# One of two subtractions of the query items handed from VectorE to ScalarE and GpSimd, in eight items of a transformer block

## The chip, the cores and the metric

The kernel runs on one core of a Trainium2 chip. The metric is the device time of one execution in microseconds (us); a time without more words is the median of several runs. The core has five engines that run side by side, each through its own instructions in order: TensorE (PE; its weight loads are shown apart as PEld), VectorE (DVE), ScalarE (ACT), GpSimd (POOL) and SyncE (SP), which here only issues DMAs. ScalarE issues some DMAs too. They wait for one another by semaphores.

## What is computed

The reference is one transformer block on 2048 rows of 1024 values, in float32: a layer norm, linear attention with a learned feature map, a projection, and a ReLU network with 3584 hidden values, each with its residual. The change touches the feature map of the queries:

```python
pq = jnp.einsum("bhsd,hdf->bhsf", q, w_phi)
phi_q = jnp.concatenate([_softmax(pq, axis=-1), _softmax(-pq, axis=-1)], axis=-1)
...
num = jnp.einsum("bhqf,bhfd->bhqd", phi_q, kv)
den = jnp.einsum("bhqf,bhf->bhq", phi_q, z)[..., None] + 1e-6
```

There are 32 heads with 32 features each. A softmax over the 32 scores of a head needs exp(score - maximum), the softmax of the negated scores needs exp(minimum - score).

## The kernel before, in words

**Tiles and stages.** The rows are 16 tiles of 128. Every product is made of three matmuls (`mm3`, L182 to L184), since each operand is held as a rounded part and a rest: `Units` takes a weight from DRAM, ScalarE copies it (L125), and GpSimd or VectorE subtracts the copy from the raw weight (L129). The weights lie in a ring of ten places (`w`); a place is free when the matmuls of the last step that reads it are over. An item is one output tile of 128x512, eight steps of three matmuls. The order of items is: for each half of the tiles (0 to 7, then 8 to 15) 32 key and value items, 8 query items with s = 0 (the first 16 heads) and 8 with s = 1; then the projection of the attention (`wo_item`), and the network (`up_item`, `down_item`). The query items of the second half with s = 0 are items 80 to 87 of the program; those with s = 1 are 88 to 95.

**A query item.** `q_first` runs behind its last matmul. VectorE takes the maximum and the minimum of each head's 32 scores from PSUM (L516, L517, tile `qmx`), then writes score less maximum (L520) and minimum less score (L521) into the halves of tile `qe`, 128 x 1024, of which there are two buffers. Then come, at steps given by hand, `q_second` (ScalarE: the exponential of the whole tile, L525, and two DMAs of it to DRAM, L529, tensor `ed`), `q_third` (VectorE: sums L534 and reciprocals L535, tile `qsm`) and `q_fourth` (GpSimd: two small products, L544, tile `smq`).

**The attention.** 32 units u, each four row tiles of two heads' groups, are read back from `ed` in another order (`at_load`) and go through GpSimd, VectorE and ScalarE: `at_sums` (GpSimd, L595, tile `ez`), `at_reduce` (VectorE, L602, `qtz`), `at_cross` (ScalarE, L613), `at_den` (GpSimd, L617 and L618), `at_inverse` (VectorE, L621), `at_scale` (GpSimd, L626 for the first six units, L631 for the others), `at_turn` (VectorE, a transpose, L637). For the first six units the sums are made earlier. After two units `at_num` makes 32 short matmuls (L650), which need the transposes of both units, and ScalarE and VectorE take the result from PSUM (L657, L667). This work is spread by hand over the items from 83 on.

**What sets the order.** `when(step, f, ...)` puts a piece of work behind a step; step 8 n + k is step k of item n. At each step the pieces run in the order in which they were put there, and then `W.advance` starts the loads and splits of weights that have a free place. Every engine goes through its own instructions in exactly this order. So `q_second` of item n stands at step 6 of item n + 1, `q_third` at step 3 of item n + 2, `q_fourth` at step 3 of item n + 3. Of the units, `at_scale` of units 0, 1 and 2 stands at step 4 of item 85, step 5 of item 86 and step 7 of item 87, that of unit 3 at step 0 of item 89; `at_num` of the first pair stands at step 5 of item 88.

**A ring of weights.** While item 87 runs, the weights of the items with s = 1 come into the ring: step k of item 87 frees the place for weight k + 2, and ScalarE (L125) and GpSimd (L129) make it. Item 88 reads weight k at its step k, its rest first in the matmul of L183. The weights of the projection follow with a slower pace, by turns from GpSimd and VectorE (L129 both).

Of the kernel before, what the change touches and what calls it, by code (L numbers as in the profile page):

```python
# [11 lines left out]
AF = mybir.ActivationFunctionType  # L12
ALU = mybir.AluOpType
AX = mybir.AxisListType

P = 128
# [6 lines left out]
HT = NT // 2  # L23
# [117 lines left out]
def kernel(  # L141
# [12 lines left out]
    v, act, pool, pe, sp = nc.vector, nc.scalar, nc.gpsimd, nc.tensor, nc.sync  # L154
# [34 lines left out]
    def do(n, k, f, *args):  # L189
        at[n, k].append((f, args))  # L190
# [230 lines left out]
    e_of, v_of, phi_of, kv_ps, kd_of = {}, {}, {}, {}, {}  # L421
# [85 lines left out]
    def q_item(s, t, keys):  # L507
        ps = yield from project(t, keys)
        q_first(s, t, ps)

    def q_first(s, t, ps):

        pq = ps.rearrange("p (h f) -> p h f", f=32)
        pa = ps.rearrange("p (a c f) -> p a c f", a=4, c=4)
        m = pqp.tile([P, 2, 16], F32, name="qmx", bufs=2)
        v.tensor_reduce(out=m[:, 0, :], in_=pq, op=ALU.max, axis=AX.X)  # L516
        v.tensor_reduce(out=m[:, 1, :], in_=pq, op=ALU.min, axis=AX.X)  # L517
        e = pqp.tile([P, 4, 2, 4, 32], F32, name="qe", bufs=2)
        m = m.rearrange("p s (a c) -> p s a c", a=4)
        v.tensor_sub(e[:, :, 0], pa, m[:, 0, :, :, None].to_broadcast([P, 4, 4, 32]))  # L520
        v.tensor_sub(e[:, :, 1], m[:, 1, :, :, None].to_broadcast([P, 4, 4, 32]), pa)  # L521
        e_of[s, t] = e

    def q_second(s, t):
        act.activation(e_of[s, t], e_of[s, t], AF.Exp)  # L525
        b, i = place_of[t]
        dst = ed[b].rearrange("a i (g s t) (n x) -> s (i g) (t n) a x", g=2, s=2, n=4)
        for sd in range(2):
            act.dma_start(dst[sd, i, :, 4 * s:4 * s + 4], e_of[s, t].rearrange("p a s c f -> s p a (c f)")[sd])  # L529
# [417 lines left out]
    def item(gen, *args, keys):  # L947
        items.append((gen, args + (keys,)))
        steps.extend((k,) for k in keys)
        return len(items) - 1  # L950
# [11 lines left out]
    for b, tiles in enumerate(groups):  # L962
        for hf in range(2):

            pairs = b == 0 and hf == 0
            for j in range(0, 4, 2 if pairs else 1):
# [3 lines left out]
                for half in range(2):  # L970
                    n = item(wo_pair, tiles[j:j + 2], hf, half, keys=[("wo", hf, 4 * half + k // 2) for k in range(8)])
# [26 lines left out]
    def when(step, f, *args):  # L998

        if step < 8 * first_up:  # L1000
            do(step // 8, step % 8, f, *args)
        else:
            do(first_up + (step - 8 * first_up) // 4, step % 4, f, *args)
# [4 lines left out]
    for t in range(1, NT):  # L1008
        n = t - 1 if t < HT else q_n[1, t - HT] + 1
# [104 lines left out]

    a0 = last_kv + 6
    for (sl, t), n in q_n.items():
        when(8 * n + 14, q_second, sl, t)
        when(8 * n + 19, q_third, sl, t)
        when(8 * n + 27, q_fourth, sl, t)
        b, i = place_of[t]  # L1120
        if (sl, i) == (1, 3):
            when(8 * n + 34, sm_store, b)
            when(8 * n + (48, 48, 48, 72)[b], sm_load, b)
# [88 lines left out]
    for b in range(2):  # L1212
        for m in DOWN:
            n = down_n[b, m, NP - 1] + 1
# [110 lines left out]
```

## Time and profile before

| | us |
|---|---|
| median of 3 runs | 1872.5 (1872.37 to 1872.6) |
| the profiled execution | 1870.48 |
| its span, first to last instruction | 1868.7 |
| mean granted clock of TensorE | 0.999 of full speed |

A line of a timeline gives the start in us, the duration, the engine, the line of the kernel, the operation, what it writes and reads, and how many instructions are merged; in brackets stands how long the engine was idle before, and what released it. A line of the waits names who waited for whom: us in total, times, the longest. A line of the stretches has for each engine the busy us and in brackets the instructions, then the granted clock, the DMAs' busy share and GB/s. The durations of matmuls overlap, since the next one starts before the one ahead has ended; what counts is the distance of their starts.

### The profile page before, as it was taken

To read this page: it belongs to the slowest core of one execution; us is meant where nothing else is said; L and a number is where in the kernel's file an instruction comes from. 1 tells how busy PE (TensorE), PEld (TensorE's weight loads), DVE (VectorE), ACT (ScalarE), POOL (GpSimd) and SP (SyncE) were. 2 spreads that over 40 slices of the span, in tenths; PEclk is the share of its full clock that TensorE was granted. 3 is DMA by queue.
4 is the path that set the end of the run, shared out by engine and by line. 5 is a ranking of instruction groups with operands and counts; after the bars stand their busy time and mean duration, and the time that the engine had idled before them with its cause. 6 is when DMAs were issued, how large, how long until landed. Compare 5 with 4: busy or idle time off the path is not lost.

```text
span 1868.7 us, 28840 instructions
## 1 busy us (share of the span) xinstructions
PE 1856.5 (99%) x10064; PEld 1516.3 (81%) x10064; DVE 1063.8 (57%) x1655; ACT 770.5 (41%) x1379; POOL 979.0 (52%) x991
## 2 busy tenths in 40 slices
PE   9999999999999999999999999999999999999999
PEld 7777788888887777888888888888888888888887
DVE  7787678677689878575555653443433333343333
ACT  5322245233333333354455554444444444444442
POOL 4887745888947988343333222222344444444443
PEclk9999999999999999999999999999999999999999
DMA  7988798666575676887888975666677677777765
GB/s 229 286 294 288 231 289 270 190 203 202 178 227 181 223 243 203 280 278 232 247 262 259 324 249 184 193 201 205 225 223 215 216 218 239 238 215 217 216 216 177
DMA packets 333635, 433.04 MB, mean 232 GB/s; under 512 B 28720, under 2 KB 194608, under 8 KB 333488
## 3 DMA queue, kind: packets, MB, share of 16 engines
q1 hardware_dynamic: 299696, 414.41, 70.1%
q10 hardware_dynamic: 33792, 16.78, 3.2%
q8 instruction: 79, 1.29, 0.3%
q14 instruction: 68, 0.56, 0.1%
HBM read 293.21 MB, written 137.89 MB: 231 GB/s over the span
## 4 chain that ended last, share of the span: by engine, by line
PE 93%; DVE 3%; POOL 1%; issue 1%; ACT 0%; DMA 0%; SPq 0%; ACTq 0%; DVEq 0%; POOLq 0%
PE mm L182 24%; PE mm L183 24%; PE mm L184 24%; PE ac L182 4%; PE ac L184 4%; PE ac L183 4%; PE tp L184 2%; PE tp L183 2%; PE tp L182 2%; PE tp L246 1%; PE ac L465 1%; PE ac L650 1%; DVE qsm L534 0%; DVE qe L637 0%; POOL w L129 0%
## 5 line engine op out<-in xcount | busy, mean ns | idle before, releaser
L129 POOL TENSOR_TENSOR w<-raw,w 128x512 fp32r<-128x512 f32 x353 | 469.0, 1331 | 698.3 <-ACT w L125 663.2
L125 ACT ACTIVATE w<-raw 128x512 fp32r<-128x512 f32 x686 | 409.4, 626 | 508.8 <-PE mm L184 232.4
L129 DVE TENSOR_TENSOR w<-raw,w 128x512 fp32r<-128x512 f32 x333 | 271.0, 815 | 511.6 <-ACT w L125 507.6
L182 PE MATMUL mm<-w,xT 128*128 128x512 f32 x768 | 306.0, 398 | 0.0
L183 PE MATMUL mm<-w,xT 128*128 128x512 f32 x768 | 300.2, 391 | 0.4 <-POOL w L401 0.4
L184 PE MATMUL mm<-w,xT 128*128 128x512 f32 x768 | 299.6, 390 | 0.0
L182 PE MATMUL mm<-hT,w 128*128 128x512 f32 x672 | 261.5, 389 | 0.0
L183 PE MATMUL mm<-hT,w 128*128 128x512 f32 x672 | 261.5, 389 | 0.0
L184 PE MATMUL mm<-hT,w 128*128 128x512 f32 x672 | 261.5, 389 | 0.0
L182 PEld LDWEIGHTS mm<-w,xT 128*128 128x128 f32 x768 | 144.4, 188 | 35.2 <-issue 4.1
L184 PEld LDWEIGHTS mm<-w,xT 128*128 128x128 f32 x768 | 144.4, 188 | 30.9
L363 POOL TENSOR_TENSOR b<-b 128x256 f32<-128x256 f32 x176 | 143.6, 816 | 48.0 <-DMA b<-in_w_dram 38.6
L183 PEld LDWEIGHTS mm<-w,xT 128*128 128x128 f32 x768 | 144.6, 188 | 29.2 <-POOL w L401 1.0
L184 PE MATMUL mm<-w 128*128 128x512 f32 x392 | 152.6, 389 | 0.0
L182 PE MATMUL mm<-w 128*128 128x512 f32 x392 | 152.6, 389 | 0.0
L183 PE MATMUL mm<-w 128*128 128x512 f32 x392 | 152.6, 389 | 0.0
L182 PEld LDWEIGHTS mm<-hT,w 128*128 128x128 f32 x672 | 126.2, 188 | 26.4
L183 PEld LDWEIGHTS mm<-hT,w 128*128 128x128 f32 x672 | 126.2, 188 | 26.2
L184 PEld LDWEIGHTS mm<-hT,w 128*128 128x128 f32 x672 | 126.2, 188 | 26.0
L183 PEld LDWEIGHTS mm<-w 128*128 128x128 f32 x392 | 73.6, 188 | 15.3
L184 PEld LDWEIGHTS mm<-w 128*128 128x128 f32 x392 | 73.6, 188 | 15.2
L182 PEld LDWEIGHTS mm<-w 128*128 128x128 f32 x392 | 73.6, 188 | 15.3
(173 smaller groups left out, 3106.0 us busy)
## 6 DMA issues: line engine op xcount, KB each, us to landing
raw<-t SPq DMA_DIRECT2D x224, 256.0 KB, 3.9
raw<-ad SPq DMA_DIRECT2D x196, 256.0 KB, 3.0
raw<-in_w_dram SPq DMA_DIRECT2D x168, 256.0 KB, 3.1
ad<-c SPq DMA_DIRECT2D x112, 256.0 KB, 3.6
b<-in_w_dram SPq DMA_DIRECT2D x44, 512.0 KB, 5.8
t<-b SPq DMA_DIRECT2D x44, 512.0 KB, 5.0
ad<-s SPq DMA_DIRECT2D x84, 256.0 KB, 4.1
ed<-qe ACTq DMA_DIRECT2D x64, 256.0 KB, 4.1
```

Source lines behind the costliest of these rows:

```text
L125: nc.scalar.activation(w[:, 0, :], raw[1], AF.Copy)
L129: eng.tensor_tensor(out=w[:, 1, :], in0=raw[1], in1=w[:, 0, :].bitcast(F32), op=ALU.subtract)
L182: pe.matmul(ps, a_hi, b_hi, start=first, stop=False, skip_group_check=more)
L183: pe.matmul(ps, a_hi, b_lo, start=False, stop=False, skip_group_check=more)
L184: pe.matmul(ps, a_lo, b_hi, start=False, stop=last, skip_group_check=more)
L246: pe.transpose(pt[:, k, :], xn[:, (4 * j + k) * P:(4 * j + k + 1) * P], ident)
L363: pool.tensor_tensor(out=tsum[*u, *out], in0=tsum[*u, *a], in1=tsum[*u, *b], op=ALU.subtract)
L465: pe.matmul(kv_ps[s][g][32 * i:32 * (i + 1), 0:64], vt[:, 32 * h:32 * (h + 1)], phi[:, 64 * h:64 * (h + 1)], start=first, stop=last)
L650: pe.matmul(banks[g][32 * c:32 * (c + 1), 256 * j:256 * (j + 1)], kvL[rows, 2 * q + h // 4, 32 * (h % 4):32 * (h % 4 + 1)], phT_of[u - 1 + ...
```

## The change

In the items 80 to 87 VectorE no longer makes minimum less score. ScalarE copies the scores from PSUM into the second half of `qe` with factor -1, behind the other instructions of `q_first`. GpSimd then adds the minimum, repeated over the 32 features, in place. This addition is a new piece `q_min`, at step 8 n + 12, that is at step 4 of item n + 1, two steps ahead of the exponential. At that step it is put ahead of what other loops put there and ahead of the weights that the step frees. The eight other items of the second half, and all of the first half, stay as they are.

```diff
         v.tensor_sub(e[:, :, 0], pa, m[:, 0, :, :, None].to_broadcast([P, 4, 4, 32]))
-        v.tensor_sub(e[:, :, 1], m[:, 1, :, :, None].to_broadcast([P, 4, 4, 32]), pa)
         e_of[s, t] = e
+        if t >= HT and s == 0:
+            act.activation(e[:, :, 1], pa, AF.Copy, scale=-1.0)
+            qm_of[t] = m
+        else:
+            v.tensor_sub(e[:, :, 1], m[:, 1, :, :, None].to_broadcast([P, 4, 4, 32]), pa)
+
+    qm_of = {}
+
+    def q_min(t):
+        e = e_of[0, t][:, :, 1]
+        pool.tensor_tensor(out=e, in0=e, in1=qm_of.pop(t)[:, 1, :, :, None].to_broadcast([P, 4, 4, 32]), op=ALU.add)
...
     for (sl, t), n in q_n.items():
+        if t >= HT and sl == 0:
+            when(8 * n + 12, q_min, t)
         when(8 * n + 14, q_second, sl, t)
```

## The prediction

> **What bounds the kernel now.** I read the page first: the span, TensorE's busy share, the chain that ended last.
>
> ```profile
> span 1868.7 us, 28840 instructions
> ...
> PE 1856.5 (99%) x10064; PEld 1516.3 (81%) x10064; DVE 1063.8 (57%) x1655; ACT 770.5 (41%) x1379; POOL 979.0 (52%) x991
> ...
> PE 93%; DVE 3%; POOL 1%; issue 1%; ACT 0%; DMA 0%; SPq 0%; ACTq 0%; DVEq 0%; POOLq 0%
> ```
>
> TensorE is busy for 1856.5 of 1868.7 us, so 12.2 us are all that any change beside the matmuls can win back, plus what a lowered clock costs. The waits of TensorE, the second view, say whose they are.
>
> ```profile
> PE ac L650 <- DVE qe L637: 2.8, 2, 2.4
> ...
> PE mm L183 <- POOL wf L129: 1.5, 1, 1.5
> ```
>
> The longest single wait is 2.4 us: the matmuls of `at_num` (L650) wait for a transpose by VectorE (L637). Third view: the timeline of TensorE around it, with an undisturbed `at_num` above it to compare.
>
> ```profile
> 578.81 1.09 PE L650 MATMUL ac<-qe,kvL 64*32 64x256 f32 x32
> 579.83 0.50 PE L182 MATMUL mm<-w,xT 128*128 128x512 f32 x1
> ...
> 581.10 0.39 PE L184 MATMUL mm<-w,xT 128*128 128x512 f32 x1
> ...
> 588.90 0.66 PE L650 MATMUL ac<-qe,kvL 64*32 64x256 f32 x16
> 591.94 1.11 PE L650 MATMUL ac<-qe,kvL 64*32 64x256 f32 x16 [2.38 <-DVE qe L637]
> 592.98 0.80 PE L182 MATMUL mm<-w,xT 128*128 128x512 f32 x1
> ...
> 595.17 0.39 PE L184 MATMUL mm<-w,xT 128*128 128x512 f32 x1
> ```
>
> Undisturbed, the first matmul after the 32 short ones starts 1.02 us after them (579.83 less 578.81). Here it starts 4.08 us after (592.98 less 588.90): 3.06 us late. From that matmul to the sixth one it takes 2.19 us in place of 1.27: 0.92 more. The whole event costs 3.06 + 0.92 = 3.98 us, the most that a relieved VectorE could win here. Fourth view: busy time by stretch.
>
> ```profile
> 508.00:549.00 41.00, 41.00 (x210) 33.34 (x209) 32.98 (x51) 12.96 (x17) 17.97 (x24) 1.00 0.66 204
> 552.40:588.90 36.50, 36.50 (x216) 28.70 (x214) 36.33 (x54) 11.75 (x21) 23.52 (x31) 1.00 0.66 207
> ...
> 591.70:593.40 1.70, 1.46 (x17) 0.65 (x18) 1.70 (x5) 0.32 (x1) 1.57 (x2) 0.50 0.68 186
> 593.40:595.10 1.70, 1.70 (x5) 1.31 (x5) 1.70 (x4) 1.28 (x3) 1.11 (x2) 0.52 0.46 122
> 595.10:597.00 1.90, 1.90 (x9) 1.53 (x9) 1.90 (x4) 1.26 (x5) 1.90 (x2) 1.00 0.00 0
> ```
>
> The columns are PE, PEld, DVE, ACT, POOL, then the granted clock. VectorE has 8.0 us of idle time from 508 to 549 (41.00 less 32.98) and practically none from 552.4 to 588.9 (36.33 of 36.50): in the second stretch it is behind, and whatever moves its start moves the transpose for which TensorE waits. The clock is at 0.50 to 0.52 for some 3.4 us after the gap.
>
> **Where the change lies in this.** The eight items are the first-half columns (s = 0) of tiles 8 to 15, items 80 to 87 in program order. Counting `qmx` reductions back from the last one, item 87 is the one below at 546.50, so all eight lie in the first stretch, where VectorE has slack. What it loses there it would have idled. The question is what reaches 552.32, where VectorE's last idle time ends.
>
> ```profile
> 546.50 0.69 DVE L516 TENSOR_REDUCE qmx<-mm 128x16 f32<-128x512 f32 x1 [0.34 <-PE mm L184]
> ...
> 548.90 1.22 DVE L534 TENSOR_REDUCE qsm<-qe 128x32 f32<-128x1024 f32 x1
> ...
> 552.32 1.25 DVE L637 STREAM_TRANSPOSE qe<-qe 128x1024 f32<-128x1024 f32 x1 [1.81 <-POOL qe L626]
> ...
> 557.05 2.09 DVE L129 TENSOR_TENSOR w<-raw,w 128x512 fp32r<-128x512 f32 x1
> 559.06 1.21 DVE L534 TENSOR_REDUCE qsm<-qe 128x32 f32<-128x1024 f32 x1
> ...
> 560.57 1.19 DVE L637 STREAM_TRANSPOSE qe<-qe 128x1024 f32<-128x1024 f32 x1
> ```
>
> At 552.32 VectorE had waited 1.81 us for GpSimd's L626 (`at_scale` of unit 2). So the stage that ends in TensorE's wait starts from GpSimd, the engine that the change loads.
>
> **The change part by part.** Durations of the nearest operations, from the view of tile qe:
>
> ```profile
> L595 POOL TENSOR_TENSOR ez<-qe,zb x52: 1267/1292/1873, 561.8 to 736.0; 128x512 f32<-128x512 f32 x52
> ...
> L521 DVE TENSOR_TENSOR qe<-qmx,mm x32: 668/677/680, 224.6 to 603.6; 128x512 f32<-128x512 f32 x32
> ...
> L626 POOL TENSOR_TENSOR qe<-qe,smx x6: 1907/1918/1921, 529.2 to 566.1; 128x1024 f32<-128x1024 f32 x6
> ```
>
> Removed: eight times L521, 0.68 us each (0.60 from start to start). That is 8 x 0.60 = 4.8 us of VectorE, worth 0 at the end: each ends in an idle time of VectorE before 552.32.
>
> Added on ScalarE: eight copies of 128x512 from PSUM. The nearest row is L657 below, 1.09 us for two, so 0.55 each. Added on GpSimd: eight additions of 128x512 in place with a value repeated along the last axis. L626 has the same kind of operand and twice the elements: 0.96 is the lower end. L595 has as many elements, its second operand repeated over another axis: 1.29, and 1.87 in its worst case. I take 1.05, near L626, since the operands are alike.
>
> Now the queues at items 86 to 88. GpSimd and ScalarE:
>
> ```profile
> 542.51 3.80 POOL L129 TENSOR_TENSOR w<-raw,w 128x512 fp32r<-128x512 f32 x3 [5.97 <-ACT w L125]
> 546.28 0.40 POOL L544 TENSOR_TENSOR smq<-qsm 128x16 f32<-128x16 f32 x2
> 546.64 3.77 POOL L129 TENSOR_TENSOR w<-raw,w 128x512 fp32r<-128x512 f32 x3
> 550.38 1.91 POOL L626 TENSOR_TENSOR qe<-qe,smx 128x1024 f32<-128x1024 f32 x1
> 552.25 0.40 POOL L544 TENSOR_TENSOR smq<-qsm 128x16 f32<-128x16 f32 x2
> 555.42 1.30 POOL L129 TENSOR_TENSOR w<-raw,w 128x512 fp32r<-128x512 f32 x1 [2.77 <-ACT w L125]
> 556.67 1.92 POOL L626 TENSOR_TENSOR qe<-qe,smx 128x1024 f32<-128x1024 f32 x1
> ```
>
> ```profile
> 541.80 4.03 ACT L125 ACTIVATE w<-raw 128x512 fp32r<-128x512 f32 x6 [2.60 <-PE mm L184]
> 545.74 1.05 ACT L525 ACTIVATE qe<-qe 128x1024 f32<-128x1024 f32 x1
> ...
> 551.67 1.09 ACT L657 ACTIVATE oT<-ac 128x512 fp32r<-128x512 f32 x2 [4.88 <-PE ac L650]
> ...
> 553.74 0.93 ACTq L529 DMA_DIRECT2D ed<-qe  x2
> 554.71 1.15 ACT L125 ACTIVATE w<-raw 128x512 fp32r<-128x512 f32 x2 [1.00 <-DMA qe<-ed]
> ```
>
> Items 80 to 85: their additions fall into GpSimd's idle time (23 of 41 us in the first stretch). An addition starts when the second reduction ends and ends about when the removed subtraction would have, so the exponential moves by some tenths of a us, and nothing waits for it before the sums (L534) one item later. Items 80 and 81 are later by 2 us, also absorbed.
>
> Item 86: its copy fits ahead of the six L125 (ScalarE idled 2.60 us before 541.80). Its addition is placed at step 4 of the next item: behind L544 at 546.28 and the first of the three L129 at 546.64, ahead of the other two and of L626. It starts at 547.90, and each of these is later by 1.05. The last L129, a weight for step 7 of item 88, ends at 550.40 + 1.05 = 551.45. TensorE needs it here:
>
> ```profile
> 552.53 0.39 PE L183 MATMUL mm<-w,xT 128*128 128x512 f32 x1
> ```
>
> 1.08 us are left: cost nothing, up to an addition of 2.13 us (552.53 less 550.40). L626 ends 1.05 later, and L637 on VectorE starts at 553.37 in place of 552.32: **1.05 us late**. The exponential of item 86 moves from 545.74 to 549.0; VectorE's L534 for it moves from 548.90 to 550.1, hidden by the longer wait for L626.
>
> Item 87: its addition comes after L626 and L544, 553.7 to 554.75. Its copy stands behind the exponential of item 86 and that one's two DMA issues (0.93) and runs from 551.0 to 551.6, done when L657 at 551.67 gets what it waits for. The exponential of item 87 follows its addition, 554.8 to 555.85, then its DMA issues to 556.8 and the two L125 (1.15) to 558.0 (before: to 555.85). VectorE reaches its L129 at 558.1, in place of 557.05, and finds its operand just ready. That L129 took 2.09 us, until GpSimd's L626 (556.67 + 1.92 = 558.59) was over and half a us more; now it would meet GpSimd's L129, 557.45 to 558.70, and end at 559.25. The next L534 starts at 559.25 in place of 559.06: of the 1.05 us, 0.2 is left. GpSimd's next L626 ends at 560.6 to 561.15, and L637 of unit 3, at 560.57 before, starts at 560.8 to 561.15: 0.2 to 0.6 late. By 1.29 for the addition the same walk gives 0.75 to 1.1 late.
>
> From there VectorE never waits up to 588.9, so the transpose at the gap is late by the same. The two L637 and L129 waits behind the gap (0.4 and 1.5 us) move along with everything. **Sum:** -0 (VectorE) + 0 (ScalarE) + 0.5 (GpSimd's delay of unit 2, passed on by VectorE) = +0.5 us. The profiled execution took 1870.48 us about its span of 1868.7; with +0.5 it would be 1871.0. The median before is 1872.5, 2.0 above; with +0.5: **1873.0 us**.
>
> One cover can fail: the two buffers of `qe`. VectorE's L520 of item 88 (556.9) must wait until the DMA of item 86's exponentials has landed; they are issued at 550.1 to 551.0 in place of 546.8 to 547.7.
>
> ```profile
> ed<-qe ACTq DMA_DIRECT2D x6, 256.0 KB, 4.0
> ```
>
> This row (545 to 565 us) gives 4.0 us to landing: 555.0, 1.9 us to spare.
>
> [...]
>
> **The rivals.**
> 1. **VectorE's relief reaches the gap.** If the 1.81 us wait at 552.32 were not governed by GpSimd's order, or the L129 at 557.05 fell into a free moment and took 0.6 in place of 2.09, VectorE would be ahead at the gap. For: it is the engine that ends the wait. Against: the eight items end before 552.32. The most is 3.98: 1868.5.
> 2. **The low clock does not come, or comes later.** The gap changes by tenths of a us, and the clock fell after a gap of 2.38 only; without it 0.92 us and about 0.5 for the 16 slow short matmuls (1.11 against 0.66 busy) are saved: 1873.0 - 1.4 = 1871.6. For: the other gaps, of 0.45 and 1.5 us, kept full clock. Against: the gap grows. [...]
> 3. **Slower: a long addition and a second low stretch.** If the addition takes as long as L595's worst (1.87), unit 2 is late by 1.9 us, the gap grows to 4.3 us, and a second stretch of 3.4 us at half clock costs 1.7 more (half of 3.4): +3.6 to 4.2 with a DMA landing late, about 1876.5. It decides from an addition of some 1.8 us. With 1.29 and the second stretch it would be +2.8: 1875.3, still within 0.2%.
>
> **How the numbers follow.** Forecast (+0.2 to +1.1) 0.58; rival 1 0.06; rival 2 0.14; a second low stretch or a late DMA with an ordinary addition (+1.5 to +3) 0.12; rival 3 0.10. About 0.2% (3.7 us) is what a measurement of this kernel can tell from no change; so within it: 0.58 + 0.14 + 0.12 = 0.84; faster by more 0.06; slower by more 0.10. Range: from 1871.0 (rival 2 with nothing left of the delay: 1872.5 - 1.4 = 1871.1) to 1875.3 (1.29 with the second stretch).
>
> **What would show it.** Eight copies on ScalarE of about 0.55 us, eight additions on GpSimd of about 1.05; VectorE idle longer before 549; L637 of unit 2 near 553.4, unit 3 near 561; the gap before the second half of L650 still there, near 2.9 us, at half clock after it. Wrong if the gap shrinks (VectorE was ahead), if L183 waits for w near 552.5, or if L520 waits for ed.

## The result, and the profile after

The changed kernel takes 1875.87 us (median of 19 runs, 1873.25 to 1877.46), the kernel before 1872.71 us in the runs beside it (19 runs). The ratio is 1.0017, with an interval from 1.0011 to 1.0024: slower by 2 to 4.5 us, 3.2 in the middle. The forecast was 1873.0 with a range up to 1875.3, so the time lies above the range, though within 0.2% of the kernel before.

The waits of TensorE in the changed kernel show the same wait as before at their head, longer (lines have moved: `at_num` is L660, the transpose L647):

```profile
PE ac L660 <- DVE qe L647: 5.2, 2, 4.7
```

The timeline of TensorE around it:

```profile
589.93 0.66 PE L660 MATMUL ac<-qe,kvL 64*32 64x256 f32 x16
595.31 1.11 PE L660 MATMUL ac<-qe,kvL 64*32 64x256 f32 x16 [4.72 <-DVE qe L647]
596.35 0.80 PE L182 MATMUL mm<-w,xT 128*128 128x512 f32 x1
...
600.65 0.39 PE L183 MATMUL mm<-w,xT 128*128 128x512 f32 x1
```

The gap was 2.38 us and is 4.72. From the first matmul behind it the eleventh starts 4.30 us later (600.65 less 596.35), where an undisturbed row needs 1.27 for six and 0.23 for each of five more, 2.4: the low clock now costs 1.9, before 0.92. The stretches say the same in their clock column, the last but two:

```profile
592.00:596.00 4.00, 0.69 (x16) 0.23 (x16) 3.96 (x8) 1.96 (x5) 2.10 (x4) 0.71 0.09 26
596.00:600.00 4.00, 4.00 (x17) 2.88 (x10) 4.00 (x8) 2.51 (x7) 3.41 (x3) 0.50 0.38 107
600.00:604.00 4.00, 4.00 (x18) 3.26 (x17) 3.97 (x5) 2.98 (x5) 3.92 (x7) 0.94 0.76 164
```

A mean clock of 0.71 over 4 us means 2.3 us at half clock, so half clock begins at about 593.7; 0.94 puts its end at about 600.5. It lasts 6.8 us, twice the 3.4 us of the kernel before (about 591.6 to 595.0).

The gap's growth, 2.3 us, and the longer low clock, 1.0 us, come to 3.3 us, near the measured 3.2. That they come so near is in part chance: TensorE also reaches the gap 1.03 us later (589.93 against 588.90), and the spans differ by 5.5 us (1874.2 against 1868.7), since the profiled execution of the kernel before was 2.0 us quicker than its median; of the changed kernel it was at its median (1876.01). A better ground for the sum is the kernel with the change in items 80 to 85 alone (below), which is no slower than the kernel before and whose profile is at its median (1872.36). TensorE in it, then in the changed kernel:

```profile
591.86 0.98 PE L663 MATMUL ac<-qe,kvL 64*32 64x256 f32 x16 [2.32 <-DVE qe L650]
...
610.16 0.50 PE L183 MATMUL mm<-w,oT 128*128 128x512 f32 x1 [1.30 <-DVE w L129]
```

```profile
613.80 0.50 PE L183 MATMUL mm<-w,oT 128*128 128x512 f32 x1 [0.71 <-DVE w L129]
```

Against this kernel, TensorE restarts behind the gap 3.45 us later (595.31 less 591.86), the longer low clock adds 0.7, and a shorter wait for a weight of the projection gives back 0.5: 3.6 us later at 613.80, and 3.6 at the end (spans of 1874.2 and 1870.6).

Why is the transpose late? Durations first, in the view of tile qe: the new operations cost what was estimated (0.55 and 1.05).

```profile
L523 ACT ACTIVATE qe<-mm x8: 597/599/602, 511.3 to 553.1; 128x512 f32<-128x512 f32 x8
L532 POOL TENSOR_TENSOR qe<-qe,qmx x8: 1047/1052/1093, 514.5 to 555.5; 128x512 f32<-128x512 f32 x8
```

Their place is the surprise. ScalarE, items 86 and 87:

```profile
540.88 1.06 ACT L535 ACTIVATE qe<-qe 128x1024 f32<-128x1024 f32 x1 [1.51 <-POOL qe L532]
541.98 0.93 ACTq L539 DMA_DIRECT2D ed<-qe  x2
543.25 0.60 ACT L523 ACTIVATE qe<-mm 128x512 f32<-128x512 f32 x1 [1.30 <-DVE qe L520]
543.75 3.23 ACT L125 ACTIVATE w<-raw 128x512 fp32r<-128x512 f32 x6
550.92 1.06 ACT L535 ACTIVATE qe<-qe 128x1024 f32<-128x1024 f32 x1 [3.95 <-POOL qe L532]
...
558.71 1.15 ACT L125 ACTIVATE w<-raw 128x512 fp32r<-128x512 f32 x2 [1.00 <-DMA qe<-ed]
```

The copy of item 86 does not start when the matmuls are over, at about 541.3, but at 543.25, right behind VectorE's L520 (542.49 + 0.68 = 543.17). The six weight copies behind it start at 543.75 in place of 541.80. The wait for L520 is not the only hindrance here: the exponential of item 85, at 538.14 before, starts at 540.88, behind an addition, and its two DMA issues keep ScalarE until 542.91. GpSimd passes that on and adds its own:

```profile
544.45 3.83 POOL L129 TENSOR_TENSOR w<-raw,w 128x512 fp32r<-128x512 f32 x3 [1.71 <-ACT w L125]
...
549.80 1.08 POOL L532 TENSOR_TENSOR qe<-qe,qmx 128x512 f32<-128x512 f32 x1
550.81 2.56 POOL L129 TENSOR_TENSOR w<-raw,w 128x512 fp32r<-128x512 f32 x2
553.29 1.95 POOL L636 TENSOR_TENSOR qe<-qe,smx 128x1024 f32<-128x1024 f32 x1
```

1.94 us late at the first weight (544.45 against 542.51), 2.91 at the scaling of unit 2 (553.29 against 550.38). And VectorE:

```profile
542.49 0.68 DVE L520 TENSOR_TENSOR qe<-mm,qmx 128x512 f32<-128x512 f32 x1
...
552.01 1.22 DVE L544 TENSOR_REDUCE qsm<-qe 128x32 f32<-128x1024 f32 x1 [3.40 <-ACT qe L535]
...
555.27 1.25 DVE L647 STREAM_TRANSPOSE qe<-qe 128x1024 f32<-128x1024 f32 x1 [1.66 <-POOL qe L636]
...
560.01 1.26 DVE L129 TENSOR_TENSOR w<-raw,w 128x512 fp32r<-128x512 f32 x1
...
563.08 1.25 DVE L647 STREAM_TRANSPOSE qe<-qe 128x1024 f32<-128x1024 f32 x1 [0.29 <-POOL qe L636]
...
570.05 0.69 DVE L520 TENSOR_TENSOR qe<-mm,qmx 128x512 f32<-128x512 f32 x1 [0.72 <-DMA ed<-qe]
...
594.07 1.19 DVE L647 STREAM_TRANSPOSE qe<-qe 128x1024 f32<-128x1024 f32 x1
```

The transpose at the gap was here in the kernel before:

```profile
590.70 1.19 DVE L637 STREAM_TRANSPOSE qe<-qe 128x1024 f32<-128x1024 f32 x1
```

Against before, the transposes are late by 2.95 (unit 2), 2.5 (unit 3, since L129 now takes 1.26 in place of 2.09) and 3.37 (the one at the gap, behind a wait of 0.72, in which L520 of item 90 waits for the DMA of item 88's exponentials). Some 0.2 us of each is older: this execution is 0.22 behind at the last reduction of item 87 (546.72 against 546.50).

**The theory.** The copy is held behind VectorE's three readings of the same scores, as if the two engines could read the PSUM tile `mm` only in turn (it starts 0.08 us after the last of the three ends). Being in front of the weight copies on ScalarE, it holds them. **Rivals:** the eight additions and the later DMAs by themselves; the longer low clock as a cause of its own; an even share of the eight items.

### The profile page after: what moved, and what is told of

Read it like the earlier page. It is cut to its first block, busy times and chain, and to the rows that moved or that the text cites. A ratio compares the mean times of both kernels' runs of the same rounds, so it can differ in the third digit from the quotient of the medians.

```text
span 1874.2 us, 28849 instructions
## 1 busy us (share of the span) xinstructions
PE 1859.4 (99%) x10064; PEld 1517.4 (81%) x10064; DVE 1062.3 (57%) x1647; ACT 775.1 (41%) x1387; POOL 987.1 (53%) x999
## 3 DMA queue, kind: packets, MB, share of 16 engines
q8 instruction: 79, 1.29, 0.3%
## 4 chain that ended last, share of the span: by engine, by line
PE 66%; DVE 3%; POOL 1%; DMA 0%; issue 0%; ACT 0%; ACTq 0%; DVEq 0%
PE mm L182 16%; PE mm L183 16%; PE mm L184 16%; PE ac L182 4%; PE ac L184 4%; PE ac L183 4%; PE tp L184 2%; PE tp L183 2%; PE tp L182 2%; PE ac L660 1%; DMA ed<-qe 0%; DVE qtz L612 0%; DVE qe L647 0%; DVE w L129 0%; DVE qsm L544 0%
## 5 line engine op out<-in xcount | busy, mean ns | idle before, releaser
L129 POOL TENSOR_TENSOR w<-raw,w 128x512 fp32r<-128x512 f32 x353 | 471.3, 1337 | 697.7 <-ACT w L125 654.5
L125 ACT ACTIVATE w<-raw 128x512 fp32r<-128x512 f32 x686 | 409.0, 626 | 504.7 <-PE mm L184 224.7
L129 DVE TENSOR_TENSOR w<-raw,w 128x512 fp32r<-128x512 f32 x333 | 273.2, 821 | 510.9 <-ACT w L125 502.4
```

What stands on the lines that cost most here:

```text
L125: nc.scalar.activation(w[:, 0, :], raw[1], AF.Copy)
L129: eng.tensor_tensor(out=w[:, 1, :], in0=raw[1], in1=w[:, 0, :].bitcast(F32), op=ALU.subtract)
```

## Experiments

Times of the kernel before are those of the runs beside each, 1872.2 to 1872.7. Each kernel writes `moved(s, t)` for the condition of the change; only what else differs is shown.

**One item or eight.** The change in item 86 alone.

```diff
-        if t >= HT and s == 0:
+        if t == 14 and s == 0:
```

> The change as it is, in item 86 alone; the seven other items keep VectorE's subtraction. Theory (one item sits in front of the refill of the weight ring): the six L125 are 1.9 us late, unit 2's transpose some 2.9 us late, the time 2 to 3.3 us above the kernel before (1874.7 to 1876). Rival (the eight items share the cost evenly): 0.4 us above, 1873.1.

Measured: 1874.71 us, ratio 1.0014 (1.0005 to 1.0023), 2.2 us. TensorE restarts behind a gap of 3.62:

```profile
594.40 1.08 PE L663 MATMUL ac<-qe,kvL 64*32 64x256 f32 x16 [3.62 <-DVE qe L650]
```

One item makes two thirds of the cost. The even share (0.4 us) is out. ScalarE, then VectorE in this kernel:

```profile
543.47 0.60 ACT L523 ACTIVATE qe<-mm 128x512 f32<-128x512 f32 x1 [4.11 <-PE mm L184]
```

```profile
560.22 0.68 DVE L129 TENSOR_TENSOR w<-raw,w 128x512 fp32r<-128x512 f32 x1
...
562.33 1.19 DVE L650 STREAM_TRANSPOSE qe<-qe 128x1024 f32<-128x1024 f32 x1
```

ScalarE has been free since 540.32 here, and the copy still starts only behind L520, which ends at 543.10; the view names TensorE as the releaser, but its matmuls were over at about 541.2. So the wait for VectorE is enough to hold the copy. Unit 2 is late by 3.17 (555.49 against 552.32), L129 gives back 1.41 of it, and unit 3 is late by 1.76.

**The six items ahead.** Items 80 to 85 alone.

```diff
+        if HT <= t < 14 and s == 0:
```

> The change in items 80 to 85 alone. Theory: VectorE only idles more, GpSimd has room, nothing reaches unit 2's transpose: within 0.4 us of the kernel before (1872.3 to 1873.1). Rival (even share): six eighths of 3.2, 2.4 us above, 1875.1.

Measured: 1872.51 us, ratio 1.0000 (0.9991 to 1.0009). No difference, as forecast for these items, though the even share would have wanted 2.4. VectorE, in this kernel:

```profile
552.96 1.25 DVE L650 STREAM_TRANSPOSE qe<-qe 128x1024 f32<-128x1024 f32 x1 [2.48 <-POOL qe L639]
...
557.69 1.36 DVE L129 TENSOR_TENSOR w<-raw,w 128x512 fp32r<-128x512 f32 x1
...
560.49 1.19 DVE L650 STREAM_TRANSPOSE qe<-qe 128x1024 f32<-128x1024 f32 x1
```

Unit 2 is 0.64 us late, since the later exponential of item 85 and its DMA issues still delay the first weight copies (542.41 against 541.80); but L129, which took 2.09, now takes 1.36, and unit 3 is not late (560.49 against 560.57). The wait in that L129 works as a buffer.

**The copy first.** All eight items, ScalarE's copy issued ahead of VectorE's reductions.

```diff
+        act.activation(e[:, :, 1], pa, AF.Copy, scale=-1.0)
         v.tensor_reduce(out=m[:, 0, :], in_=pq, op=ALU.max, axis=AX.X)
         v.tensor_reduce(out=m[:, 1, :], in_=pq, op=ALU.min, axis=AX.X)
```

> All eight items as in the change, but ScalarE's copy is issued ahead of the two reductions, so that it doesn't stand behind VectorE's L520 on the same tile. Theory (the copy waited for L520, and so held the six weight copies behind it back by 1.9 us): the copy of item 86 starts when its last matmul ends, the six L125 start within 0.3 us of where they did before, unit 2's transpose is 1.0 to 1.3 us late in place of 2.95, and the time is 0 to 1.5 us above the kernel before (1872.7 to 1874.2). Rival (GpSimd's eight additions and the later DMAs are the cost): as the changed kernel, 3 us above, 1875.9.

Measured: 1879.84 us, ratio 1.0041 (1.0028 to 1.0054): 7.3 us slower. Neither forecast. VectorE in this kernel:

```profile
543.90 0.69 DVE L519 TENSOR_REDUCE qmx<-mm 128x16 f32<-128x512 f32 x1 [2.02 <-ACT qe L518]
```

The first reduction, which writes only `qmx`, waits for the copy, which writes `qe`. All that the two share is the tile `mm` in PSUM that they read. So in this program reading one PSUM tile is enough to make one engine wait for the other, 2.02 us here; sharing the tile `qe`, which the expectation blamed, is not needed. And now a ring closes: the copy of an item stands behind the exponential of the item ahead, that waits for GpSimd's addition, that for VectorE, and VectorE for the copy. The six weight copies start at 549.19, though some 2.7 us of that is this execution's own: its mean clock is 0.997, in the other profiles 0.998 or more, and its 1882.2 us are 2.4 above the median.

```profile
549.19 3.22 ACT L125 ACTIVATE w<-raw 128x512 fp32r<-128x512 f32 x6
```

This waiting could have been read before the forecast. The waits of the kernel before hold a row of the key items, where a copy of the values (L427) and the reductions (L430) read the two halves of one tile `mm`:

```profile
DVE kmx L430 <- ACT vt L427: 52.6, 41, 2.5
```

The reductions waited 41 times, for 52.6 us in all. What happens without the waiting was not tried.

**The copy later.** All eight items, the copy issued just ahead of the addition, and so behind four of the six weight copies in item 86.

```diff
     def q_min(s, t):
         e = e_of[s, t][:, :, 1]
+        m, pa = qm_of.pop((s, t))
+        act.activation(e, pa, AF.Copy, scale=-1.0)
         pool.tensor_tensor(out=e, in0=e, in1=m[:, 1, :, :, None].to_broadcast([P, 4, 4, 32]), op=ALU.add)
```

> All eight items of the change, with only the place of ScalarE's copy changed: it is issued at step 4 of the next item, just ahead of GpSimd's addition, and so behind four of the six weight copies in item 86. Theory (the failing step was the place of the copy, which cannot run before L520 and holds the L125 behind it): the first L125 of the six start where they did before, unit 2's transpose is some 1.05 us late as forecast for the change, and the time is 0 to 1.3 us above the kernel before (1872.6 to 1873.9). Rival (the later exponentials and their DMAs, and eight additions, cost the 3 us, not the copy's place): 1875 to 1876.5, as the change.

Measured: 1873.95 us against 1872.19, ratio 1.0009 (1.0000 to 1.0018): 0.05 above the theory's end, and more than a us below the rival's. Against the runs beside it that is 1.8 us more, half a us above the theory's 0 to 1.3, and the interval, 0 to 3.4, does not shut out the rival. The trace decides. ScalarE and VectorE:

```profile
542.17 2.66 ACT L125 ACTIVATE w<-raw 128x512 fp32r<-128x512 f32 x4 [1.00 <-PE mm L184]
```

```profile
553.72 1.25 DVE L651 STREAM_TRANSPOSE qe<-qe 128x1024 f32<-128x1024 f32 x1 [1.67 <-POOL qe L640]
...
561.52 1.25 DVE L651 STREAM_TRANSPOSE qe<-qe 128x1024 f32<-128x1024 f32 x1 [0.29 <-POOL qe L640]
```

```profile
593.26 0.82 PE L664 MATMUL ac<-qe,kvL 64*32 64x256 f32 x16 [3.29 <-DVE qe L651]
```

This execution is some 0.4 us behind (its gap opens at 589.31 against 588.90). Less that, unit 2 is 1.0 us late and unit 3 0.55: the prediction's 1.05 and 0.2 to 0.6. The gap grows by 0.9, of which 0.21 is again the wait of item 90's L520 for a DMA, and half clock is over by 597.13, at most 3.9 us behind the restart (from 594.61 to 596.75 the matmuls start 0.43 us apart, from 597.13 on 0.23). So the walk through GpSimd's and VectorE's queues held as far as unit 3, with the additions and the later DMAs in place; the place of the copy is what the prediction had wrong. Why the time is 1.8 us above and not 0.5 is settled only in part.

**Copy and addition apart,** in item 86: the copy without the addition (its exponentials are then those of the negated scores without the minimum), and the addition of a tiny number with VectorE's subtraction kept.

```diff
-        if moved(sl, t):
-            when(8 * n + 12, q_min, sl, t)
```

> Item 86 alone, with ScalarE's negated copy behind L520 as in the change, and without GpSimd's addition, so that this item's second half is the exponential of the negated score without the minimum; VectorE's subtraction is gone in it. Theory (the copy's wait holds the six weight copies behind it): the six L125 and all on GpSimd behind them 1.9 us late, unit 2's transpose 1.9 us late, the time 0.8 to 1.9 us above the kernel before (1873.4 to 1874.5). Rival (only the addition costs): no difference, 1872.3 to 1872.9.

```diff
-        in1=qm_of.pop((s, t))[:, 1, :, :, None].to_broadcast([P, 4, 4, 32])
+        in1=eps_of[0][:, :, None, None].to_broadcast([P, 4, 4, 32])
```

> Item 86 alone, with VectorE's subtraction kept and GpSimd's addition put at the same place, adding 0.0000005 in place of the minimum; no copy on ScalarE. Theory: the six L125 stay in place, unit 2's transpose is 1.05 us late, of which VectorE's wait in L129 gives some back: 0 to 0.8 us above the kernel before (1872.5 to 1873.3). Rival (the addition is the cost of item 86): 2 us above, 1874.7, as with the whole change in item 86.

Measured: 1873.80 us, ratio 1.0006 (0.9997 to 1.0015), and 1872.45, ratio 0.9999 (0.9990 to 1.0007). VectorE with the copy alone, then with the addition alone:

```profile
554.39 1.25 DVE L650 STREAM_TRANSPOSE qe<-qe 128x1024 f32<-128x1024 f32 x1 [3.81 <-POOL qe L639]
...
559.12 0.67 DVE L129 TENSOR_TENSOR w<-raw,w 128x512 fp32r<-128x512 f32 x1
...
561.23 1.19 DVE L650 STREAM_TRANSPOSE qe<-qe 128x1024 f32<-128x1024 f32 x1
```

```profile
553.83 1.25 DVE L647 STREAM_TRANSPOSE qe<-qe 128x1024 f32<-128x1024 f32 x1 [1.67 <-POOL qe L636]
...
558.56 1.01 DVE L129 TENSOR_TENSOR w<-raw,w 128x512 fp32r<-128x512 f32 x1
```

The copy makes unit 2 late by 2.07, but L129 gives back 1.42 of it (0.67 in place of 2.09): unit 3 is 0.66 late. The addition makes it late by 1.5, of which 0.5 is older (its six L125 start at 542.29 against 541.80), and L129 gives back 1.08. Neither alone is told from no change with certainty (the gaps are 2.79 and 3.00 us, the latter with 0.58 of item 90's wait for a DMA); the buffer in L129, 1.4 us, swallows most of either. Together, in item 86 alone, they made unit 2 late by 3.17 and overflowed it, with 1.76 left: that is why the two do not add up.

**Item 87 alone.**

```diff
+        if t == 15 and s == 0:
```

> The change as it is, in item 87 alone. Theory: its copy has nothing urgent behind it, its addition comes behind unit 2's scaling; the exponential and the next weight copies on ScalarE are 1 to 2 us later, so that VectorE's L129 may meet GpSimd's L129 in place of its longer L626 and wait up to 0.7 us less: 0.8 us below to 0.4 above the kernel before (1871.7 to 1872.9). Rival (the rest of the change's 3.2 us, beside the 2.2 of item 86, is made in item 87): 1 us above, 1873.5.

Measured: 1873.59 us, ratio 1.0004 (0.9995 to 1.0013). In the trace the next weight copies on ScalarE follow the exponential at 556.15 in place of 554.71, VectorE's L129 takes 1.26, the transpose of unit 3 waits 0.29 us for GpSimd, and L520 of item 90 waits 1.19 us for the DMA of item 88's exponentials, which was issued from 558.65 to 559.65, 8.3 us or more before the wait ends; in the kernel before it lands 4.2 to 4.7 us after its issues:

```profile
567.97 0.69 DVE L520 TENSOR_TENSOR qe<-mm,qmx 128x512 f32<-128x512 f32 x1 [1.19 <-DMA ed<-qe]
```

The middle is nearer to the rival, and the gap grows to 3.29, but the interval takes in no change. The DMA wait is real in the profile and is of the kind that the prediction named as a cover that can fail, but it named item 88, and the wait comes at item 90. Why this DMA lands so late was not tried.

**The hand-over where VectorE is behind.** The items 88 to 95 in place of 80 to 87, with the copy first and with the copy last.

```diff
-        if t >= HT and s == 0:
+        if t >= HT and s == 1:
```

> The same hand-over, with the copy issued first, in the other eight query items of the second half (88 to 95), of which six lie in the stretch in which VectorE never waits, ahead of the gap. Theory (the stretch up to the gap is VectorE's): VectorE does 0.6 us less for each of some six items, the gap of 2.4 us shrinks by 2 us or more, and the time falls by 2 to 4 us (1868.7 to 1870.7). Rival (GpSimd sets the pace there too, since each addition stands ahead of sums and scalings of the units): 0 to 3 us above the kernel before.

> The hand-over in items 88 to 95 as in the run before it, but with the copy issued behind VectorE's L520, as the change has it. [...] Rival (GpSimd's additions hold back the sums and scalings of the units, whatever the copy does): 0 to 4 us above.

Measured: 1876.71 us, ratio 1.0025 (1.0015 to 1.0035), and 1876.18, ratio 1.0018 (1.0009 to 1.0027). The first is above both of its forecasts; the second has the time of the rival, not the 1868.5 to 1871.5 us that the author expected of a relieved VectorE. With the copy first VectorE waits for it, 7.4 us in six items:

```profile
DVE qmx L519 <- ACT qe L518: 7.4, 6, 1.9
```

With the copy last it does not, and the gap shrinks to 0.28 us, under the 1 us expected; but the win is given back at the first weights of the projection:

```profile
590.23 0.67 PE L663 MATMUL ac<-qe,kvL 64*32 64x256 f32 x16 [0.28 <-DVE qe L650]
...
604.19 0.50 PE L183 MATMUL mm<-w,oT 128*128 128x512 f32 x1 [2.59 <-POOL w L129]
...
607.73 0.50 PE L182 MATMUL mm<-w,oT 128*128 128x512 f32 x1 [0.75 <-ACT w L125]
...
609.08 0.60 PE L183 MATMUL mm<-w,oT 128*128 128x512 f32 x1 [0.84 <-POOL w L129]
```

It is a fault of the same kind as in item 86: on ScalarE the weight copies stand behind the copies and exponentials of items 93 to 95, and these wait in turn for GpSimd's addition (2.33 us ahead of the exponential at 601.18) and for VectorE's L520 (2.69 us ahead of the copy at 606.57). Behind these waits the clock is at half: from 609.48 to 612.04 the matmuls start 0.43 us apart, in place of 0.23, until the 32 short ones at 612.60, which take 1.12 us in all, nearly as undisturbed. A later transpose is waited for too, 2.6 us.

**Without those three.** Items 88 to 92, and 88 to 91, copy last.

```diff
+        if HT <= t < 13 and s == 1:
```

> The hand-over in items 88 to 92 alone, copy behind L520. In the run with all eight of this half the gap shrank to 0.28 us, and matmuls of the projection waited 2.6, 0.75 and 0.8 us for weights whose copies stood on ScalarE behind the copies and exponentials of items 93 to 95. Theory (that was the price of items 93 to 95): the gap stays under 0.5 us, the weights' copies are free again, and the time is 1.5 to 3.5 us below the kernel before (1869 to 1871). Rival (what is won at the gap is waited for at the next weights anyway, since VectorE and GpSimd make them and are no further ahead): within 0.7 us of the kernel before.

> The hand-over in items 88 to 91 alone, copy behind L520. Theory: VectorE is 0.6 us less ahead than with five items, the gap 0.3 to 1 us, the clock stays at full speed, and the time is 1 to 3 us below the kernel before (1869.5 to 1871.7). Rival: within 0.7 us of the kernel before.

Measured: 1869.68 us against 1872.56, ratio 0.9985 (0.9976 to 0.9994), **2.9 us faster**, and 1871.68, ratio 0.9995 (0.9987 to 1.0004). The second cannot be told from no change. With five items the gap is 0.87 us, not under the 0.5 expected, and the clock does not fall (1.00 behind the gap, and 1.000 in the mean of the profiled execution); with four it is 1.47 and the clock stays at 1.00 there, from 588 to 600, but weights are waited for at 607.6 and 609.4 (1.06 and 1.29 us), and behind these two waits the clock is at half: the 32 short matmuls at 610.54 take 1.96 us, undisturbed 1.09. The first, then the second:

```profile
590.99 0.67 PE L663 MATMUL ac<-qe,kvL 64*32 64x256 f32 x16 [0.87 <-DVE qe L650]
```

```profile
592.00:596.00 4.00, 4.00 (x19) 3.31 (x18) 4.00 (x8) 2.33 (x8) 4.00 (x4) 1.00 0.30 85
```

```profile
591.35 0.67 PE L663 MATMUL ac<-qe,kvL 64*32 64x256 f32 x16 [1.47 <-DVE qe L650]
```

So, in these runs, the same hand-over pays where VectorE is behind and ScalarE has nothing urgent queued. The kernel with items 88 to 92 is the fastest here.

## Why the prediction was wrong, point by point

- **What bounds the kernel: right.** The gap at L650 is where the time went, and by VectorE's transposes.
- **Nothing won in items 80 to 87: right where it was tried.** Items 80 to 85 alone made no difference (1872.51 us).
- **"the exponential moves by some tenths of a us": wrong.** In items 80 to 85 it starts 2.3 to 4.2 us later, since each addition waits for a copy that stands behind L520. This is absorbed up to item 85, whose exponential and DMA issues then keep ScalarE until 542.91, in the very idle time that the next step counted on.
- **Durations: right.** 0.60 for a copy, 1.05 for an addition.
- **The step that failed: "its copy fits ahead of the six L125 (ScalarE idled 2.60 us before 541.80)".** The copy was taken to start with VectorE's reductions. It starts behind L520, 1.9 us later, and pushes the six L125 from 541.80 to 543.75. Unit 2 is late by 2.95 in place of 1.05. Moving the copy behind four of these brings the forecast's numbers for the two transposes (1.0 and 0.55) and 1873.95 us.
- **"1.08 us are left" for the weight of step 7: failed with it.** TensorE waits 0.26 us for it in the changed kernel, one of the prediction's own signs of being wrong. That costs nothing at the end, since TensorE waits later at the gap anyway, whose end VectorE sets.

```profile
553.42 0.50 PE L183 MATMUL mm<-w,xT 128*128 128x512 f32 x1 [0.26 <-POOL w L129]
```

- **The wait in L129 as a cover: right in kind.** It gives back up to 1.4 us, in the copy-alone run; in the changed kernel only 0.83, because there the later exponential of item 87 delays the weight copies too.
- **The DMA cover: right in kind, wrong in place.** The prediction looked for the wait at L520 of item 88 and took 4.0 us to landing; it comes at item 90, 0.72 us in the changed kernel, where the second DMA of item 88 takes 8.2 us to landing. With it "From there VectorE never waits" failed too.
- **The clock: rival 2 wrong, the second low stretch right.** It was given 0.12 with an ordinary addition, "+1.5 to +3", and came, just above that, by another way than a long addition. 0.7 to 1.0 of the 3.2 us is its part. The low stretch lasted 6.83 us in place of 3.41 and ended 5.4 us later than before (600.5 against 595.0), so it came on top of the delay. The clock fell 0.3 us ahead of TensorE's restart before (591.6) and 1.7 ahead of it now (593.6).

**What stays open.** The kernel before ran its profiled execution 2.0 us under its median; the run of items 80 to 85, whose profile was at the median, has a wait of TensorE of 1.3 us for a weight of the projection that the former lacks, and six other kernels here have one of 1.0 to 1.3 us, but that this is the difference was only seen in single executions. How the cost of item 87 alone (0.9 us in the middle, with an interval that takes in no change) divides was not settled either.

## What to carry to other kernels

Before an operation is handed to another engine, look at what it reads: in this program a second engine on the same PSUM tile did not run beside the first but behind it (2.0 us of waiting with the copy first, a start 0.08 us behind L520 in the change), and whatever stands behind it on its own engine waits too. Then look at whether the engine that is relieved is behind at that place or idle, and whether the two that take over have something urgent queued there; the same change was 3.2 us slower in one set of items and 2.9 us faster in another. A delay smaller than the waits on its way can vanish, so costs found one by one need not add up.

## What the runs showed of the hardware that was not expected

- **A PSUM tile read by two engines in turn.** In the copy-first kernel a reduction with no other tile in common waits 2.0 us for ScalarE's copy, and in the changed kernel the copy starts 0.08 us after L520 ends.
- **The clock and the gap.** By the clock column half clock lasted 3.4 us behind gaps of 2.32 to 3.62 us, in six kernels, and 6.83 us, twice that, in the changed kernel, behind a gap of 4.72. A gap's length alone does not decide: 2.32 and 2.38 us brought the clock down, while in the run of items 88 to 95 with the copy last a wait of 2.59 us (ahead of 604.19) left the matmuls behind it 0.23 us apart, as at full clock, and two shorter ones, 0.75 and 0.84 us, had half clock behind them. In the run of items 88 to 91 half clock came behind waits of 1.06 and 1.29 us. In the profiles of the kernel before and of the changed kernel the fall came 587.1 us after the clock had first come up. What decides was not shown. With 6.8 us at half clock behind the gap of 4.72 and none behind the one of 0.87, the difference between the two gaps is worth more than its own length.
- **VectorE beside GpSimd.** The same VectorE operation L129 took 0.67, 1.01, 1.26, 1.36 or 2.09 us: where one of GpSimd's long instructions (L129, 1.30 us, or the scaling, 1.92) ran at its start, it ended 0.54 to 0.56 us behind that instruction's end, and where only GpSimd's two short products did, it took 0.67 and 0.68 (the copy alone, item 86 alone). The GpSimd instruction that came next to it took up to half a us longer (2.37 in place of 1.92, in the run of item 87 alone).
